# Attention, then a low-rank mixer and an MLP: where the mixing factor is loaded from, how the gains reach the q copy, and the order of the first batch

## The chip, the cores and the metric

The kernel runs on one core of a Trainium2 chip. The metric is the device time of one execution in microseconds (us), median of several runs. Every run in this document was in the fast state; even so the mean granted clock of single executions lies between 0.987 and 1.000, which matters below. A profile is of one execution; its span is some 1.8 us shorter than the time. Ratios are the mean time of one kernel's fast runs over that of the kernel before's fast runs in the same rounds, so they are not quite the ratio of the medians quoted beside them.

PE is TensorE, DVE is VectorE, ACT is ScalarE, POOL is GpSimd, SP is SyncE; SPq and POOLq are their instruction queues. A "group" is four heads (loads of q, k and v), a "pair" two heads; a batch has 12 heads, so 3 groups and 6 pairs. Tile names in the profiles: `ph` and `po` are the two matmuls of the MLP, `pm` and `px` the mixing.

## The reference

```python
q_n, k_n = rmsnorm(q, g_q), rmsnorm(k, g_k)            # q, k, v: 8 x 12 x 448 x 64
attn = softmax(q_n @ k_n^T / sqrt(64)) @ v
x = attn with the heads side by side                   # 8 x 448 x 768
u = x + (x^T @ U @ V)^T                                # U: 448 x 32, V: 32 x 448
out = u + relu(u @ w_ch1) @ w_ch2                      # 768 x 3072, 3072 x 768
```

Inputs and outputs are float32; the kernel multiplies in bfloat16.

## The kernel before

PE is to be busy all the time: while the MLP of batch b runs, the attention of batch b+1 is woven between its matmuls. Before the first MLP there is nothing to weave with, so batch 0 has a hand-made order, the "head": a string of words, each one step (`SC20` scores of pair 2, block 0; `X20` its exponential; `V20` its product with v; `N20` the normalization; `R2`, `q2`, `S2` reduce, rsqrt and scaling; `sq` squares; `w10` the first of six chunks of w_ch1; `late` the block below). Every engine does its steps in that order.

```python
def setup_late():                                      # all on POOL
    nc.gpsimd.tensor_copy(Us, Uf...)                   # U and V to bfloat16
    nc.gpsimd.tensor_copy(V4..., Vf...)
    nc.gpsimd.tensor_copy(Vsh[:, 0, 0:64], V4[:, 384:448])
    nc.gpsimd.tensor_copy(Vsh[:, 1, 64:128], V4[:, 0:64])
# [...]
def load_mix(part):
    if part == "U":
        nc.gpsimd.dma_start(Uf, moe_U...)
    else:                                              # V four times, one below the other, by one DMA
        nc.gpsimd.dma_start(Vf, bass.AP(moe_V.tensor, moe_V.offset, [[0, 4], [S, rank], [1, S]]))
# [...]
def take_q(p, pt):                                     # PSUM to SBUF, times the product of the gains
    nc.vector.tensor_scalar(blocks(p)[:, :, 0], pt[:, 0], gg, None, OP.mult)
# [...]  the middle of the head: V is sent at ld:V; late, sq5 and cast1 stand in a row on POOL; V20 needs cast1
#   ... X01 SC02 ld:V T1:0 X02 Eq1 ... X21 S3 T3:0 R4 q4 SC22 N00 X22 V10:1 late SC23 Eq3
#   V11:2 sq5:p Ek3:v cast1 SC30 S4 pU:0 N11 X23 SC31 X30 T4:2 SC32 N10 X31 V20:1 ...
# [...]  in the attention of batch 1 (pairs 6 to 11), for the pairs of batch 2:
if p == 9:   add(0, touch, 6); add(0, load, 6); add(0, load_v, 6)        # group 6 = pairs 12, 13
if p == 10:  add(0, squares, 12); add(0, squares, 13)                    # POOL
if p == 11:  add(0, reduce, 12); add(0, reduce, 13)                      # DVE, behind the first head of pair 10, ahead of the other three of pairs 10 and 11
```

(The last three lines are the effect of a longer set of conditions.) The weights are six chunks of w_ch1, then six of w_ch2 (three of its first half, three of its second), all sent by POOL, 0.79 MB each as written.

Of the kernel before, what the change touches and what calls it, by code (L numbers as in the profile page):

```python
# [17 lines left out]
def kernel(  # L18
# [60 lines left out]
    V4 = consts.tile([P, S], BF16, name="V4")  # L79
    Vsh = consts.tile([P, 2, P], BF16, name="Vsh")  # L80
    gg = consts.tile([P, 1], FP32, name="gg")
    grow = consts.tile([1, 4, D], FP32, name="grow")
    one = consts.tile([1, 1], FP32, name="one")
    eps = consts.tile([SP, 1], FP32, name="eps")
    rk0 = consts.tile([SP, 8], FP32, name="rk0")
    NE, NV, NQ, NWARM = 2, 3, 4, 11
    Es = [consts.tile([SP, 2, PAD + NJ * S + PAD], BF16, name=f"E{i}") for i in range(NE)]
    vas = [consts.tile([SP, HG, NJ, D + 1], BF16, name=f"va{i}") for i in range(NV)]

# [26 lines left out]
    def setup():  # L116
        nc.vector.memset(xss[1], 0.0)
        nc.gpsimd.memset(eps, D * 1e-6)
        nc.gpsimd.memset(one, 1.0)
        for i, g in enumerate((g_q, g_k)):  # L120
            nc.gpsimd.dma_start(grow[:, i], g.rearrange("(o d) -> o d", o=1))
        nc.gpsimd.memset(shift, 0.0)
        make_identity(nc, ident)
        for t in Es:
            nc.gpsimd.memset(t[:, :, 0:PAD], 0.0)
            nc.gpsimd.memset(t[:, :, PAD + NJ * S:], 0.0)
        for t in vas:
            nc.gpsimd.memset(t[:, :, :, D:D + 1], 1.0)
        for t in qkTs:
            nc.gpsimd.memset(t[:, SQK:], 0.0)  # L130
        nc.gpsimd.memset(Vsh, 0.0)

    def setup_late():
        nc.gpsimd.tensor_copy(Us, Uf.rearrange("p (j r) -> p j r", j=NJ))
        nc.gpsimd.tensor_copy(V4.rearrange("r (j p) -> r j p", j=NJ), Vf.rearrange("r (p j) -> r j p", j=NJ))
        nc.gpsimd.tensor_copy(Vsh[:, 0, 0:64], V4[:, 384:448])
        nc.gpsimd.tensor_copy(Vsh[:, 1, 64:128], V4[:, 0:64])

    def gain_row():

        nc.vector.tensor_tensor(grow[:, 2:4], grow[:, 0:1].to_broadcast([1, 2, D]),
                                grow[:, 1:2].to_broadcast([1, 2, D]), OP.mult)

    def gain(column):

        nc.tensor.matmul(column, grow[:, 2:4].rearrange("o h d -> o (h d)"), one, start=True, stop=True)

    def load_mix(part):
        if part == "U":
            nc.gpsimd.dma_start(Uf, moe_U.rearrange("(p j) r -> p (j r)", j=NJ))  # L150
        else:
            nc.gpsimd.dma_start(Vf, bass.AP(moe_V.tensor, moe_V.offset, [[0, 4], [S, rank], [1, S]]))

    def setup_U(pU):
        for par in range(2):
# [32 lines left out]
    def load(t):  # L188
        for a in range(2):
            for s in range(2):  # L190
                load_pair(nc.sync, t, s, a)
# [49 lines left out]
    def blocks(p):  # L241
        return qkTs[p % NQ][:, 0:SQK].rearrange("p (j s r) -> p j s r", j=NJ, s=2)
# [4 lines left out]
                                ident[:SP, :SP])  # L247

    def take_q(p, pt):
        nc.vector.tensor_scalar(blocks(p)[:, :, 0], pt[:, 0], gg, None, OP.mult)  # L250

    def take_k(p, pt, copy=nc.vector.tensor_copy, js=slice(0, NJ)):
        copy(k_side(p)[:, 0:SQK].rearrange("p (j s r) -> p j s r", j=NJ, s=2)[:, js, 1], pt[:, 1, js])
# [261 lines left out]
    def begin(hcs, dcs):  # L515
# [15 lines left out]


    HEAD = """
        sq00:a sq01:a R00 q00 R01 rk00 q01 sq1:a gg G ld:U Sq00 Sq01 GC rk01 Tq0:0 F4:1 sq2:a
        Sk0 Tk0:1 F2:2 Ek0:a R1 Sl0 Tl0:2 q1 Eq0 SC00 El0:v sq3:p S1 cast0 R2 X00 SC01 F2:0 X01
        SC02 ld:V T1:0 X02 Eq1 SC03 F2:1 Ek1:v SC10 F1:0 q2 X03 X10 S2 SC11 sq4:p T2:0 R3 X11 q3
        SC12 V01:1 Ek2:v X12 SC13 V00:2 Eq2 SC20 w10 X13 SC21 w11 N01 X20 X21 S3 T3:0 R4 q4 SC22
        N00 X22 V10:1 late SC23 Eq3 V11:2 sq5:p Ek3:v cast1 SC30 S4 pU:0 N11 X23 SC31 X30 T4:2
        SC32 N10 X31 V20:1 Ub:a X32 R5 w12 Eq4 Ek4:v SC33 V21:0 X33 MT1:2 N20 q5 t1:v SC40 MT0:1
        V30:2 cast2 t0:a X40 N21 SC41 S5 V31:0 N30 SC42 N31 T5:1 X41 SC43 w13 X42 w14 sq6:p  # L540
        MU1:0 Ek5:v MU0:2 Eq5 SC50 u1:v MT2:1 X43 u0:a X50 R6 SC51 MT3:0 t3:v V40:2 SC52 sq7:p
        t2:v X51 X52 MU3:0 SC53 N40 V41:1 B10 w15 X53 R7 w20 MU2:2 N41 B11 q6 B00 S7 V51:1 u3:a
        w21 u2:a V50:0 N51 N50 MT4:2 B01 S6 B12 t4:a B02 MT5:0 MU4:1 t5:a B03 MU5:0 B13 u4:v B04
        B14 u5:v B05 B15
    """

    def head():
# [18 lines left out]
        def op(name, p, n, how):  # L566
# [11 lines left out]
            elif name == "q" and p == 0:  # L578
                nc.scalar.activation(rs0[n], rs0[n], AF.Ln, bias=eps)
                nc.scalar.activation(rs0[n][:, 0:4], rs0[n][:, 0:4], AF.Exp, scale=-0.5)  # L580
            elif name == "rk":
                nc.scalar.activation(rk0[:, 4 * n:4 * n + 4], rs0[n][:, 4:8], AF.Exp, scale=-0.5)
            elif name == "q":
                rsqrt(p, 2 if p == 6 else 1)
            elif name == "S":
                scale(p)
            elif name in ("Sq", "Sk", "Sl"):
                if 0 not in qkns:
                    qkns[0] = norm.tile([SP, NJ, 4, D], BF16, tag="qkn", name="qkn", bufs=3)
                if name == "Sq":  # L590
                    nc.vector.tensor_tensor(qkns[0][:, :, n], raw0(0)[:, :, n],
                                            rs0[n][:, 0:4].rearrange("p j -> p j ()").to_broadcast([SP, NJ, D]),
                                            OP.mult)
                else:
                    js = FIRST if name == "Sk" else REST
                    rk = rk0.rearrange("p (h j) -> p j h ()", j=NJ)[:, js]
                    nc.gpsimd.tensor_tensor(qkns[0][:, js, 2:4], raw0(1)[:, js],
                                            rk.to_broadcast([SP, js.stop - js.start, 2, D]), OP.mult)
            elif name == "T":
                hold(("T", p), how, SQK, BF16)  # L600
                for s in range(2):
                    turn(p, s, turned(("T", p)))
                del qkns[p]
            elif name == "Tq":
                hold(("Tq", 0), how, SQK, BF16)
                turn(0, 0, turned(("Tq", 0)))
            elif name in ("Tk", "Tl"):
                hold((name, 0), how, SQK, BF16)
                turn(0, 1, turned((name, 0)), (0,) if name == "Tk" else range(1, NJ))
            elif name == "Eq":  # L610
                take_q(p, turned(("T" if p else "Tq", p)))
            elif name in ("Ek", "El"):
                js = slice(0, NJ) if p else FIRST if name == "Ek" else REST
                take_k(p, turned(("T" if p else "T" + name[1], p)), copies[how], js)
            elif name == "SC":
                scores(p, (n,))
            elif name == "X":
                expo(p, n)
            elif name == "V":
                products(p, n, hold(("V", p, n), how, 4 * (D + 1)).rearrange("p (i d) -> p i d", i=4))  # L620
            elif name == "N":
                normalize(p, n, held["V", p, n].rearrange("p (i d) -> p i d", i=4))
            elif name == "MT":
                mix_to(hold(("MT", p), how, P), 0, slice(p * P, (p + 1) * P))
            elif name == "t":
                copies[how](t_of(0)[:, p * P:(p + 1) * P], held["MT", p])
            elif name == "MU":
                mix_u(p, hold(("MU", p), how, 384))
            elif name == "u":
                copies[how](u_tile(0)[:, p, :], held["MU", p])  # L630
            elif name == "pU":
                setup_U(hold("pU", how, 8 * rank).rearrange("p (a i r) -> p a i r", a=2, i=4))
            elif name == "Ub":
                copies[how](Ub, held["pU"].rearrange("p (a i r) -> p a i r", a=2, i=4))
            elif name == "B":
                begin(range(2 * p, 2 * p + 2), (n,))
            elif name == "F":
                heat(p, banks[int(how)])
            elif name == "w":
                if p == 1:  # L640
                    load_w1(n)
                else:
                    load_w2(0, n)
            elif name == "cast":
                cast_v(p)
            elif name == "gg":
                gain_row()
            elif name == "G":
                gain(warm[:, 1, 0:1])
                heat(2, warm[:, 0, :])  # L650
            elif name == "GC":
                nc.scalar.copy(gg, warm[:, 1, 0:1])  # L652
            elif name == "ld":
                load_mix(how)
            elif name == "late":
                setup_late()

# [13 lines left out]
    with tc.manual_schedule():  # L671
# [7 lines left out]
        load(1)  # L679
        load_v(0)  # L680
        load(2)
        load_v(1)
        load_v(2)
        setup()
# [68 lines left out]
```

## Time and profile before

| | us |
|---|---|
| time, median of 4 runs beside the changed kernel | 598.01 (597.3 to 598.39) |
| span of the profiled execution | 596.9 |
| first exponential starts | 10.62 |
| last exponential of batch 0 ends | 40.7 |
| first ph matmul (MLP of batch 0) | 46.52 |
| first mixing matmul of batch 1 | 95.11 |
| first ph matmul of batch 1 | 109.11 |

How to read it: PE is busy 97% of the span, so only what happens before its steady state can be shortened. The "first ph matmul" of a batch is a milestone in PE's order. The prediction below shows the lines for the stretch up to 46.52. The q copy, by its tile (least, median and most ns; first and last start):

```profile
L250 DVE TENSOR_SCALAR qkT<-bank,gg x6: 441/442/442, 9.6 to 35.4; 128x448 bf16<-128x448 bf16 x6
```

Second, the DMA queues in the two stretches from 75 to 85 us (q0: POOL's queue, the weights; q1: SP's; packets, MB, share):

```profile
q0 software_dynamic: 1237, 0.94, 120.9%
q1 hardware_dynamic: 43, 0.04, 3.3%
...
q1 hardware_dynamic: 1459, 1.42, 83.7%
q0 software_dynamic: 172, 0.12, 16.3%
```

From 75 to 80 the weights have the engines almost to themselves; by 80 they are all but through, and only then SP's loads of group 6 (sent at 78.23 to 80.23) run, almost alone: its last k lands 5.4 us after being sent, at 85.1. In this kernel the two miss each other.

### The profile page before, as it was taken

How to read it: one execution, taken by the hardware profiler on the slowest of the kernel's cores; microseconds unless marked ns; L12 is line 12 of the kernel's file. 1: busy time of each engine (PE TensorE's matmuls, PEld its weight loads, DVE VectorE, ACT ScalarE, POOL GpSimd, SP SyncE). 2: the span in 40 equal slices, each digit the busy share in tenths (PEclk: the TensorE clock that was granted, in tenths of full speed). 3: DMA queues.
4: the chain of work that ended last, by engine and by line, in shares of the span. 5: the costliest groups of instructions: out<-in, count | busy, mean ns of one | idle time of the engine just before them, and what ended most of it. 6: DMA issues, size and time to landing. Idle time of an engine off the chain costs nothing.

```text
span 596.9 us, 11275 instructions
## 1 busy us (share of the span) xinstructions
PE 581.9 (97%) x4699; PEld 319.4 (54%) x4720; DVE 297.4 (50%) x602; ACT 263.6 (44%) x426; POOL 126.5 (21%) x112
## 2 busy tenths in 40 slices
PE   7699999999999999999999999999999999999996
PEld 2465556444565555544565556544465555654563
DVE  5775867555443566454453665545454362521111
ACT  6666541566503772175610875056630476112200
POOL 6693132333030330220230131303303000000000
PEclk9979999999999999999999999999999999999999
DMA  9999993944343544553253652832445310150021
GB/s 285 253 234 238 205 231 109 235 138 126 71 137 87 138 138 130 125 136 87 77 166 68 156 142 46 201 96 84 137 124 99 69 25 9 41 94 0 1 54 53
DMA packets 107859, 72.27 MB, mean 121 GB/s; under 512 B 56676, under 2 KB 104164, under 8 KB 107808
## 3 DMA queue, kind: packets, MB, share of 16 engines
q1 hardware_dynamic: 96016, 61.30, 40.3%
q0 software_dynamic: 11232, 9.73, 10.0%
q8 instruction: 37, 0.61, 0.4%
q10 hardware_dynamic: 560, 0.52, 0.3%
q14 instruction: 14, 0.11, 0.1%
HBM read 56.78 MB, written 11.01 MB: 114 GB/s over the span
## 4 chain that ended last, share of the span: by engine, by line
PE 93%; DMA 3%; POOL 1%; ACT 1%; issue 0%; DVE 0%; SPq 0%; POOLq 0%; DVEq 0%
PE po L413 37%; PE ph L393 36%; PE sc L278 7%; PE o L291 7%; DMA Vf<-in_moe_V_dram 2%; DMA qk<-in_k_dram 2%; PE px L363 1%; PE bank L291 1%; PE sc L523 1%; PE pm L338 1%; POOL w2b L217 1%; ACT E L283 0%; PE pt L246 0%; ACT hT L396 0%; POOL va L203 0%
## 5 line engine op out<-in xcount | busy, mean ns | idle before, releaser
L283 ACT ACTIVATE E<-sc 112x896 bf16<-112x896 f32 x192 | 172.1, 914 | 162.8 <-PE sc L278 162.8
L413 PE MATMUL po<-w2b,hT 128*128 128x384 bf16 x1344 | 238.3, 326 | 0.0
L413 PEld LDWEIGHTS <-hT 128*128 128x128 bf16 x1344 | 126.4, 98 | 87.6 <-issue 9.2
L393 PEld LDWEIGHTS <-w1b 128*128 128x128 bf16 x1128 | 102.7, 98 | 105.2 <-issue 19.3
L217 POOL TENSOR_TENSOR sq<-qk 112x1024 f32<-112x1024 f32 x42 | 79.3, 1896 | 312.0 <-DMA qk<-in_k_dram 233.3
L393 PE MATMUL ph<-uB,w1b 128*128 128x512 bf16 x556 | 131.4, 379 | 1.1
L396 ACT ACTIVATE hT<-ph 128x512 bf16<-128x512 f32 (+1 forms) x122 | 66.8, 547 | 106.8 <-PE ph L393 106.4
L393 PE MATMUL ph<-uA,w1b 128*128 128x384 bf16 x552 | 100.3, 326 | 0.1
L398 DVE TENSOR_SCALAR hT<-ph 128x384 bf16<-128x384 f32 (+1 forms) x66 | 41.1, 622 | 90.5 <-PE ph L393 90.3
L291 PEld LDWEIGHTS <-E 112*128 112x128 bf16 x1536 | 62.1, 99 | 19.9 <-issue 6.8
L278 PE MATMUL sc<-qkT 64*128 64x448 bf16 x376 | 55.7, 361 | 2.0 <-ACT E L283 1.1
L291 PE MATMUL o<-va,E 112*128 112x65 bf16 x1344 | 56.9, 194 | 0.0
L231 DVE TENSOR_TENSOR qkn<-qk,rs_bank 112x1024 bf16<-112x1024 f32 x45 | 54.5, 1213 | 2.8 <-ACT rs_bank L226 2.3
L220 DVE TENSOR_REDUCE rs_bank<-sq 112x16 f32<-112x1024 f32 x43 | 52.6, 1223 | 3.4 <-ACT gg L652 1.1
L303 DVE RECIPROCAL rec<-o 128x4 f32<-128x4 f32 x84 | 15.2, 181 | 72.6 <-PE o L291 72.2
L417 DVE TENSOR_TENSOR osb<-po,xe 128x384 f32<-128x384 f32 x32 | 17.7, 557 | 40.2 <-PE po L413 39.6
L417 DVE TENSOR_TENSOR osb<-po,xo 128x384 f32<-128x384 f32 x24 | 13.4, 558 | 43.4 <-PE po L413 43.4
L278 PEld LDWEIGHTS <-qkT 64*128 64x128 bf16 (+1 forms) x384 | 13.4, 95 | 35.5 <-issue 28.8
L203 POOL CAST va<-vt 112x1024 bf16<-112x1024 f32 x23 | 23.9, 1042 | 1.2 <-DMA vt<-in_v_dram 1.2
L269 ACT ACTIVATE qkT<-qkT,gg 128x448 bf16<-128x448 bf16 x36 | 23.9, 663 | 0.0
L365 DVE TENSOR_TENSOR xe<-px,xe 128x384 bf16<-128x384 f32 x32 | 17.7, 554 | 10.1 <-PE px L363 7.1
L311 DVE TENSOR_TENSOR xe<-o,rec 64x64 bf16<-64x64 f32 x84 | 18.3, 218 | 0.7
(95 smaller groups left out, 215.3 us busy)
## 6 DMA issues: line engine op xcount, KB each, us to landing
qk<-in_q_dram SPq DMA_DIRECT2D x44, 256.0 KB, 4.3
vt<-in_v_dram SPq DMA_DIRECT2D x22, 512.0 KB, 5.8
qk<-in_k_dram SPq DMA_DIRECT2D x43, 256.0 KB, 4.7
w1b<-in_moe_w_ch_dram POOLq DMA_DIRECT2D x6, 768.0 KB, 17.9
w2b<-in_moe_w_ch_dram POOLq DMA_DIRECT2D x6, 768.0 KB, 32.4
out_dram<-osb SPq DMA_DIRECT2D x8, 336.0 KB, 2.8
out_dram<-osb SPq DMA_DIRECT2D x8, 288.0 KB, 3.0
out_dram<-osb SPq DMA_DIRECT2D x8, 240.0 KB, 2.8
```

Source lines behind the costliest of these rows:

```text
L203: nc.gpsimd.tensor_copy(vas[t % NV][:, :, :, 0:D], v_of[t][0:SP].rearrange("p h (j d) -> p h j d", d=D))
L217: nc.gpsimd.tensor_tensor(dst, src, src, OP.mult)
L220: nc.vector.tensor_reduce(rs_of(p).rearrange("p (s h j) -> p s h j", s=2, h=2)[:, :, hs], sqs[p].rearrange("p (s h j d) -> p s h j d", s=2 ...
L231: nc.vector.tensor_tensor(qkns[p].rearrange("p j g d -> p g j d"), qk_of[t][0:SP, a].rearrange("p s h (j d) -> p (s h) j d", d=D), rs_of(p ...
L278: nc.tensor.matmul(sc[0:n, hh, 0:S], flat[pp, c:c + n], blocks(p)[pp, :, 0], start=True, stop=True)
L283: nc.scalar.activation(Es[p % NE][:, :, PAD + kc * S:PAD + (kc + 1) * S], scs.pop((p, kc))[0:SP, :, 0:S], AF.Exp, scale=float(D) ** 0.5)
L291: nc.tensor.matmul(o[:, i, :], E[:, hh, c:c + P], va[:, hl, kc, :], start=(kc == 0), stop=(kc == NJ - 1))
L393: nc.tensor.matmul(ph, w1b[:, dc, hc * P:(hc + 1) * P], u[:, dc, :], start=(dc == 0), stop=(dc == KD - 1))
L396: nc.scalar.activation(hT[:, hc, 0:n], ph, AF.Relu)
L398: nc.vector.tensor_relu(hT[:, hc, 0:n], ph)
L413: nc.tensor.matmul(po, hT[:, hc, i * P:(i + 1) * P], w2b[:, half, hc], start=(hc == 0), stop=(hc == KH - 1))
L417: nc.vector.tensor_add(osb[:, hs], po, xt[i][:, hs])
```

## The change

Its intent: have V there when POOL wants it, take the small product of the gains off DVE, and reorder the head around that.

```diff
-    def load_mix(part):                                # U right after the set-up, V at ld:V, POOL's queue
-        ...one DMA each...
+    def load_mix():
+        nc.sync.dma_start(Uf, moe_U.rearrange("(p j) r -> p (j r)", j=NJ))
+        for i in range(4):
+            nc.sync.dma_start(Vf[i * rank:(i + 1) * rank], moe_V)
@@ the loads at the start
         load(2)
+        load_mix()
         load_v(1)
@@ the gains: two columns (two matmuls, one ACT copy) instead of the product of two rows on DVE
-        nc.vector.tensor_scalar(blocks(p)[:, :, 0], pt[:, 0], gg, None, OP.mult)
+        nc.vector.tensor_scalar(blocks(p)[:, :, 0], pt[:, 0], gcol[:, 0:1], gcol[:, 1:2], OP.mult, OP.mult)
@@ setup_late
+        nc.gpsimd.tensor_tensor(gg, gcol[:, 0:1], gcol[:, 1:2], OP.mult)      # for later batches
@@ HEAD: another order (cut): squares of pairs 2, 3, 4 and 5 on POOL; late and sq5 ahead of V01;
@@ cast1 ahead of S3, so that SP sends v3 and v4 ahead of the loads of group 4; one more warm-up
@@ matmul at the start, the two behind the gains gone, and the later ones placed anew
```

More of the change, by code (lines that the diff above doesn't have):

```diff
@@ L81 @@
     gg = consts.tile([P, 1], FP32, name="gg")
-    grow = consts.tile([1, 4, D], FP32, name="grow")
+    grow = consts.tile([1, 2, 2, D], FP32, name="grow")
+    gcol = consts.tile([P, 2], FP32, name="gcol")
     one = consts.tile([1, 1], FP32, name="one")
@@ L85 @@
     rk0 = consts.tile([SP, 8], FP32, name="rk0")
-    NE, NV, NQ, NWARM = 2, 3, 4, 11
+    NE, NV, NQ, NWARM = 2, 3, 4, 12
     Es = [consts.tile([SP, 2, PAD + NJ * S + PAD], BF16, name=f"E{i}") for i in range(NE)]
@@ L120, in setup @@
         for i, g in enumerate((g_q, g_k)):
-            nc.gpsimd.dma_start(grow[:, i], g.rearrange("(o d) -> o d", o=1))
+            nc.gpsimd.dma_start(grow[:, i], bass.AP(g.tensor, g.offset, [[0, 1], [0, 2], [1, D]]))
         nc.gpsimd.memset(shift, 0.0)
@@ L137, in setup_late, with gain @@
         nc.gpsimd.tensor_copy(Vsh[:, 1, 64:128], V4[:, 0:64])
-    def gain_row():
-        nc.vector.tensor_tensor(grow[:, 2:4], grow[:, 0:1].to_broadcast([1, 2, D]),
-                                grow[:, 1:2].to_broadcast([1, 2, D]), OP.mult)
-    def gain(column):
-        nc.tensor.matmul(column, grow[:, 2:4].rearrange("o h d -> o (h d)"), one, start=True, stop=True)
-    def load_mix(part):
-        if part == "U":
-            nc.gpsimd.dma_start(Uf, moe_U.rearrange("(p j) r -> p (j r)", j=NJ))
-        else:
-            nc.gpsimd.dma_start(Vf, bass.AP(moe_V.tensor, moe_V.offset, [[0, 4], [S, rank], [1, S]]))
+    def gain(columns):
+        for i in range(2):
+            nc.tensor.matmul(columns[:, i:i + 1], grow[:, i].rearrange("o h d -> o (h d)"), one, start=True, stop=True)
+    def load_mix():
+        nc.sync.dma_start(Uf, moe_U.rearrange("(p j) r -> p (j r)", j=NJ))
+        for i in range(4):
+            nc.sync.dma_start(Vf[i * rank:(i + 1) * rank], moe_V)
     def setup_U(pU):
@@ L533 @@
     HEAD = """
-        sq00:a sq01:a R00 q00 R01 rk00 q01 sq1:a gg G ld:U Sq00 Sq01 GC rk01 Tq0:0 F4:1 sq2:a
-        Sk0 Tk0:1 F2:2 Ek0:a R1 Sl0 Tl0:2 q1 Eq0 SC00 El0:v sq3:p S1 cast0 R2 X00 SC01 F2:0 X01
-        SC02 ld:V T1:0 X02 Eq1 SC03 F2:1 Ek1:v SC10 F1:0 q2 X03 X10 S2 SC11 sq4:p T2:0 R3 X11 q3
-        SC12 V01:1 Ek2:v X12 SC13 V00:2 Eq2 SC20 w10 X13 SC21 w11 N01 X20 X21 S3 T3:0 R4 q4 SC22
-        N00 X22 V10:1 late SC23 Eq3 V11:2 sq5:p Ek3:v cast1 SC30 S4 pU:0 N11 X23 SC31 X30 T4:2
-        SC32 N10 X31 V20:1 Ub:a X32 R5 w12 Eq4 Ek4:v SC33 V21:0 X33 MT1:2 N20 q5 t1:v SC40 MT0:1
-        V30:2 cast2 t0:a X40 N21 SC41 S5 V31:0 N30 SC42 N31 T5:1 X41 SC43 w13 X42 w14 sq6:p
-        MU1:0 Ek5:v MU0:2 Eq5 SC50 u1:v MT2:1 X43 u0:a X50 R6 SC51 MT3:0 t3:v V40:2 SC52 sq7:p
-        t2:v X51 X52 MU3:0 SC53 N40 V41:1 B10 w15 X53 R7 w20 MU2:2 N41 B11 q6 B00 S7 V51:1 u3:a
-        w21 u2:a V50:0 N51 N50 MT4:2 B01 S6 B12 t4:a B02 MT5:0 MU4:1 t5:a B03 MU5:0 B13 u4:v B04
-        B14 u5:v B05 B15
+        sq00:a R00 sq01:a q00 R01 q01 rk00 rk01 Sq00 G Sk0 Sq01 GC Tq0:0 Sl0 sq2:p Tk0:1 F1:2
+        Tl0:2 sq3:p sq1:a Eq0 R1 Ek0:a SC00 F3:0 El0:v q1 cast0 S1 X00 SC01 F2:0 R2 sq4:p SC02
+        T1:0 w10 X01 SC03 F3:1 X02 q2 Eq1 X03 Ek1:v w11 S2 SC10 F1:0 SC11 X10 T2:0 R3 SC12 late
+        sq5:p X11 V01:1 Ek2:v Eq2 SC13 cast1 V00:0 q3 N01 X12 X13 w12 SC20 S3 X20 w13 SC21 T3:1
+        R4 SC22 X21 sq6:p q4 V11:2 X22 SC23 Eq3 Ek3:v N00 V10:1 cast2 SC30 X23 S4 pU:0 N10 SC31
+        N11 X30 X31 T4:1 R5 Ub:a SC32 V20:2 Eq4 SC33 X32 Ek4:v X33 q5 w14 N20 V21:0 N21 MT0:1
+        SC40 X40 MT1:2 SC41 t1:a V31:0 t0:v MU0:1 S5 N31 X41 u0:v SC42 T5:2 X42 MT2:0 Eq5 SC43
+        V30:1 Ek5:v SC50 X43 R6 t2:a MU1:2 SC51 X50 sq7:p N30 V40:0 X51 SC52 X52 u1:v MT3:1
+        MU2:2 SC53 N40 X53 w15 V41:0 t3:v B10 R7 MU3:1 q6 u2:a u3:a N41 B00 V51:0 V50:2 B11
+        MT4:1 w20 B01 B12 S6 t4:a N51 MU4:0 N50 MT5:1 w21 t5:a u4:a B02 B13 MU5:1 B03 u5:a S7
+        B14 B04 B15 B05
     """
@@ L645, in op @@
                 cast_v(p)
-            elif name == "gg":
-                gain_row()
             elif name == "G":
-                gain(warm[:, 1, 0:1])
-                heat(2, warm[:, 0, :])
+                gain(warm[:, 1, 0:2])
             elif name == "GC":
-                nc.scalar.copy(gg, warm[:, 1, 0:1])
-            elif name == "ld":
-                load_mix(how)
+                nc.scalar.copy(gcol, warm[:, 1, 0:2])
             elif name == "late":
```

## The prediction

> **What bounds the kernel now.** I read the page first. TensorE (PE) is busy for 97% of the span, so nothing outside PE's own work and its few gaps can be worth much. The slices show where the exceptions lie: PEclk is below 9 only in the third slice (about 30 to 45 us).
>
> ```profile
> PE 581.9 (97%) x4699; PEld 319.4 (54%) x4720; DVE 297.4 (50%) x602; ACT 263.6 (44%) x426; POOL 126.5 (21%) x112
> ...
> PEclk9979999999999999999999999999999999999999
> ```
>
> Next I asked for the busy time of each engine in stretches of 5 us over the start. Columns: stretch, length, busy us of PE, PEld, DVE, ACT and POOL (instructions), granted clock, DMA share, GB/s. PE loses time from 20 to 30 us; from 25 to 40 us its clock is reduced, to half in one row. From 10 to 20 us ACT and DVE are each busy for over 4.6 of every 5 us. DMA has no pause.
>
> ```profile
> 10.00:15.00 5.00, 4.12 (x30) 1.80 (x32) 4.65 (x8) 4.78 (x10) 4.45 (x4) 1.00 1.10 348
> 15.00:20.00 5.00, 4.26 (x74) 2.92 (x72) 4.83 (x9) 4.74 (x9) 2.96 (x4) 1.00 1.13 298
> 20.00:25.00 5.00, 3.08 (x51) 2.12 (x48) 3.14 (x8) 4.62 (x8) 1.55 (x4) 1.00 1.16 220
> 25.00:30.00 5.00, 2.28 (x34) 1.80 (x33) 2.48 (x5) 0.71 (x1) 5.00 (x5) 0.69 1.19 239
> 30.00:35.00 5.00, 5.00 (x61) 3.17 (x58) 3.05 (x8) 3.32 (x7) 4.99 (x5) 0.50 1.18 239
> 35.00:40.00 5.00, 5.00 (x62) 2.80 (x62) 4.22 (x9) 4.10 (x7) 5.00 (x6) 0.79 1.18 246
> ```
>
> The chain of waits over the same stretch (start, length, what) names the cause. POOL sends for V at 13.35, V lands at 23.34, and POOL then does the V cast, two shifted copies, a squares product and the cast of the next v, which PE needs.
>
> ```profile
> 13.35 9.99 DMA Vf<-in_moe_V_dram
> 23.34 0.05 issue
> 23.39 0.97 POOL V L135
> ...
> 24.42 0.24 POOL Vsh L136
> 24.66 0.18 POOL Vsh L137
> 24.84 1.09 POOL w2b L217
> ...
> 26.64 1.04 POOL va L203
> 27.68 0.04 issue
> 27.72 1.04 PE bank L291 x16
> ```
>
> The list of waits gives both ends: POOL idle for 5.4 us, PE for 4.2 us (its last matmul ended at 23.56, the next began at 27.72).
>
> ```profile
> POOL V L135 <- DMA Vf<-in_moe_V_dram: 5.4, 1, 5.4
> PE bank L291 <- POOL va L203: 4.2, 1, 4.2
> ```
>
> From 46.52 us, where the first MLP proper (the ph tile) starts, PE is busy without gaps that matter. So a change of the head (batch 0 before that point) moves the end by as much as it moves this start.
>
> **What the Trainium skill says.** (1) "TensorE: Matmul & The Clock Gate", its section on why this matters for your kernels, asks for no PE-idle gaps over about 3 us, because one idle window sends the clock back to half. The trace agrees: after a gap of 4.16 us the clock is 0.50 from 30 to 35, and a group of 16 values matmuls takes 0.99 us in the chain there, 0.62 later in the head. (2) The same page (engine queue depths) has GpSimd in strict order. The trace agrees: Us, ready since 10.8 us, is cast at 17.65, and behind V everything stands. (3) "DMA: Bandwidth & Descriptors", rules for kernel authors: an outermost zero-stride dim of c copies confines a DMA to at most c engines. V's old pattern leads with 4 copies. V took 10.0 us for 224 KB, but a 256 KB load sent at 13.05 took 10.5 us on the other queue, so this trace does not show that the pattern cost anything; the backlog alone could explain it. (4) The same page says that all issuing engines share the same 16 DMA engines. So moving V to SyncE moves no work away from them; what it can buy is an earlier place.
>
> **The change part by part.**
>
> V and U on SyncE: five issues placed after the loads of group 2, before v of group 1, at some 8.5 to 11 us. The neighbours tell the landing: the last k load before them was sent at 8.11 and took 7.0 us (15.1); the v behind them 8.86 plus 7.7 (16.6). The 0.28 MB of U and V at the 350 GB/s of that stretch is 0.8 us, so V should land at about 16, and loads behind it 0.8 us later.
>
> POOL, walked in its new order (the order listing confirms it): two k scalings once rk01 is there (6.5 to 7.7), squares of pair 2 when its k has landed (8.95 to 10.85; it was on ACT), squares 3 to 12.75, cast of v0 to 13.7, squares 4 to 15.5, two w1 issues of 0.88 to 17.3, then the late block: gg, U, V and two copies, about 1.9 us, to 19.2. V, at about 16, is there: no wait. Squares 5 end at 21.1 instead of 26.7, the v1 cast at 22.1 instead of 27.7. PE needs that cast after the last exponential of pair 2, itself near 21.6. **The 4.16 us gap should go.**
>
> Cold clock: from 27.72 to 36.89 the chain holds 9.17 us of PE pieces. At warm durations from the same trace these are 4 values groups x 0.62, 5 scores x 0.30, 2 mixes x 0.17, one set of transposes 0.40 and 2 u groups x 0.33, together 5.4 us. So **3.8 us** went to the half clock. With the gap, the bound on PE's side is 4.16 + 3.8 = 8.0 us.
>
> Gains: without DVE's product (0.28 us, and 0.7 us in which PE waited for it) the columns come some 1 us sooner; an extra column matmul (its weight load about 0.18 us) costs less than that. The q copy was 442 ns over 448 columns; a second per-partition factor in the same pass should leave it there (my estimate; this trace has no such form). The first exponential is still behind q1, so behind squares of pair 1 (to 8.47) and a 1.23 us reduce: about 10.2 instead of 10.62, 0.4 us.
>
> Can ACT and DVE follow? ACT needs 24 exponentials at 0.83 us in line, 20.0; four pairs of rsqrt at 0.36 to 0.4, 1.5; Ub and two small casts, 0.8: 22.3 us from 10.2, the last exponential ending at 32.5. DVE has about as much: five reduces (1.23), five scalings (1.21), five pairs of copies (0.8), eight normalizations (0.55) and small things. Walking both in order, with R2 gating q2, R5 gating q5 (25.1) and SC50 at 29.4, I get the last exponential ending at 33.1 (40.7 before). After it come the last values, R7, S6, two normalizations, mix 5, t5, u5, four matmuls of the MLP: DVE sets this tail, 5.3 us. The MLP starts at **38.4 instead of 46.5, 8.1 us sooner**. Two different sums thus give 8.0 and 8.1; they are not independent gains to be added.
>
> Weights then become the next edge. The landings before, issue plus time: w1 chunk 0 at 29.5, chunk 1 at 35.4 (16.8 + 18.6), chunk 2 at 42.3, chunk 3 at 46.8. First uses were 40.05, 46.52, 51.4 and 57.8. The margins are 10.5, 11.1, 9.1 and 11.0 us; shifting the uses by 8 leaves 1 to 3 us. DMA is full all along, so the earlier issue of chunks 2 and on (about 22 instead of 27.6) helps little, and the loads of v3 and v4, which follow the v1 cast, come 5 us sooner and share the engines. I allow 0.5 to 1 us for waits on weights or other unforeseen ones.
>
> Sum: 598.0 - 8.1 + 0.9 = 590.8 us, 1.2% less.
>
> **The rivals.**
> A. The weights bind: chunk 0, 1 or 2 lands later than its new use. For it: the margins above, and full DMA. Against it: the bytes to be moved by then are the same. It would cost 1 to 4 us of the gain (591 to 594); a wait over some 3 us would also cool PE's clock.
> B. V still comes late, or POOL, which takes over one squares product (1.9 us) from ACT, is the bound. For it: POOL is then busy almost without pause from 9 to 32 us. Against it: its walk has the cast only 0.5 us behind the need, and V has over 1 us in hand. Cost: 1 to 3 us.
> C. ACT and DVE bind harder than walked, since each must hold over 4.6 of 5 us all through. If the MLP starts at 41, the gain is 5.5 us: 592.5.
> D. More than 8 us: over 2% needs an MLP start before 34.7 us, which the 22.3 us of ACT work plus the 5.3 us tail from 10.2 exclude (37.8 at best), unless work of later batches also shrinks; nothing there is changed but the form of six q copies.
>
> **Range and chances.** The floor is 37.8 us for the MLP start (589.2), a little below for run-to-run spread: 588.6. The top takes A or C in a strong form with part of the gain lost: 593.8. Faster by over 2% is ruled out by the ACT sum unless I misread the head (0.03); slower by over 2% would need a new stall of 20 us (0.01).
>
> **What would show it.** In the changed profile: no wait of POOL for Vf; no PE gap over 3 us between 20 and 30 and a clock of 1.00 in each 5 us row of 20 to 40; the first exponential near 10.2, the last ending near 33; the first ph matmul near 38.5; the q copy near 442 ns; no, or short, waits of PE on w1b. From there the durations of both traces should be alike. The prediction is wrong if PE waits for w1b by several us, if a new POOL or DVE wait stands where V's was, or if the later batches differ.

## The result and the profile after

The changed kernel took **593.94 us** (593.57 to 594.06, 4 runs) beside 598.01: ratio 0.9932, 95% interval 0.9915 to 0.9949. That is 4.1 us less, 0.7%, where 7.2 were predicted, and just above the top of the range (593.8). The span went from 596.9 to 592.1.

The page and the stretches of the head after:

```profile
PE 579.1 (98%) x4699; PEld 317.9 (54%) x4720; DVE 296.5 (50%) x599; ACT 263.3 (44%) x427; POOL 127.4 (22%) x112
...
PEclk9999999999999999999999999999999999999999
```

```profile
20.00:25.00 5.00, 4.44 (x84) 3.19 (x81) 4.90 (x12) 4.95 (x10) 4.99 (x5) 1.00 1.17 255
25.00:30.00 5.00, 4.89 (x82) 3.23 (x79) 4.90 (x14) 4.77 (x9) 4.73 (x5) 1.00 1.18 241
30.00:35.00 5.00, 4.96 (x84) 3.41 (x85) 4.85 (x11) 4.72 (x9) 4.39 (x5) 1.00 1.18 245
35.00:40.00 5.00, 5.00 (x50) 3.02 (x47) 2.56 (x6) 1.47 (x5) 0.00 (x0) 1.00 1.18 245
```

The gap and the cold clock are gone. POOL's timeline (start, us) has V's cast without a wait:

```profile
17.81 0.30 POOL L136 CAST Us<-Uf 112x128 bf16<-112x128 f32 x1
18.05 0.99 POOL L137 CAST V<-Vf 128x448 bf16<-128x448 f32 x1
```

The milestones of both, each taken from the timelines of PE and ACT:

| | before | after | sooner by |
|---|---|---|---|
| first ph matmul of batch 0 | 46.52 | 39.67 | 6.85 |
| first po matmul of batch 0 | 77.02 | 70.30 | 6.72 |
| first mixing matmul of batch 1 | 95.11 | 90.08 | 5.03 |
| first ph matmul of batch 1 | 109.11 | 104.08 | 5.03 |
| span | 596.9 | 592.1 | 4.8 |

So the head gave 6.85 us, and **1.7 of them were given back between 70 and 90 us**, where the kernel's program is unchanged. The chain of waits shows the place (start, length, what):

```profile
71.58 0.37 SPq L183
...
73.03 11.28 DMA qk<-in_k_dram
...
84.43 1.90 POOL sq L214
...
86.35 1.23 DVE rs_bank L217
...
88.20 0.24 DVE xe L308
...
88.49 0.69 PE o L288 x16
```

SP sends the loads of group 6 at 71.58 to 73.6, 6.6 us sooner than before. The last k of them takes 11.28 us (5.4 before) and lands at 84.3, only 0.8 us before it landed in the kernel before. POOL squares pair 13 at once, DVE reduces it at once; but in DVE's order this reduce stands ahead of the normalization that frees PE's bank, and PE waits:

```profile
PE o L288 <- DVE xe L308: 1.5, 1, 1.5
```

The DMA queues in the two stretches from 75 to 85 us (q0: POOL's queue, the weights; q1: SP's; packets, MB, share), in the same form as those of before, say why the loads take twice as long: the weights still run beside them.

```profile
q0 software_dynamic: 735, 0.56, 70.8%
q1 hardware_dynamic: 685, 0.67, 49.4%
...
q0 software_dynamic: 683, 0.52, 65.6%
q1 hardware_dynamic: 790, 0.77, 54.7%
```

### The profile page after: what moved, and what is told of

Same layout as the page of the kernel before. It is cut to its first block, busy times and chain, and to the rows that moved or that the text cites. A ratio compares the mean times of both kernels' runs of the same rounds, so it can differ in the third digit from the quotient of the medians.

```text
span 592.1 us, 11276 instructions
## 1 busy us (share of the span) xinstructions
PE 579.1 (98%) x4699; PEld 317.9 (54%) x4720; DVE 296.5 (50%) x599; ACT 263.3 (44%) x427; POOL 127.4 (22%) x112
## 4 chain that ended last, share of the span: by engine, by line
PE 91%; DMA 3%; DVE 3%; ACT 1%; issue 1%; SPq 0%; POOL 0%; DVEq 0%; POOLq 0%; ACTq 0%
PE ph L390 37%; PE po L410 36%; PE sc L275 7%; PE o L288 7%; DMA qk<-in_k_dram 2%; PE px L360 1%; DVE rs_bank L217 1%; DMA qk<-in_q_dram 1%; PE bank L288 1%; DVE qkn L228 1%; PE sc L520 1%; PE pm L335 1%; ACT E L280 0%; SPq L183 0%; ACT hT L393 0%
## 5 line engine op out<-in xcount | busy, mean ns | idle before, releaser
L288 PEld LDWEIGHTS <-E 112*128 112x128 bf16 x1536 | 60.8, 98 | 18.0 <-issue 3.2
L414 DVE TENSOR_TENSOR osb<-po,xe 128x384 f32<-128x384 f32 x32 | 17.7, 557 | 40.2 <-PE po L410 39.6
L275 PEld LDWEIGHTS <-qkT 64*128 64x128 bf16 (+1 forms) x384 | 13.3, 94 | 36.5 <-issue 28.2
L362 DVE TENSOR_TENSOR xe<-px,xe 128x384 bf16<-128x384 f32 x32 | 17.7, 554 | 10.1 <-PE px L360 7.1
```

The lines of the kernel that those rows point to most:

```text
L275: nc.tensor.matmul(sc[0:n, hh, 0:S], flat[pp, c:c + n], blocks(p)[pp, :, 0], start=True, stop=True)
L288: nc.tensor.matmul(o[:, i, :], E[:, hh, c:c + P], va[:, hl, kc, :], start=(kc == 0), stop=(kc == NJ - 1))
L414: nc.vector.tensor_add(osb[:, hs], po, xt[i][:, hs])
```

## The experiments

Sixteen runs. **Theory**: V's late landing made the gap, and loading it sooner is worth 7 to 8 us of the head by the gap and the half clock; part is lost because PE, now sooner, asks for group 6 while DMA still has weights to move. **Rivals**: the new order or the columns made the gain; the cold stretch cost nothing; the loss is due to SP's changed order (v3 and v4 ahead of group 4), to DVE's order alone, or to slow small DMAs. As the first loads arrive at different moments in different executions (the first exponential starts between 10.05 and 13.21 us in these profiles), I compare distances between milestones: from the first exponential to the first ph matmul of batch 0 (the head), and from there to the first ph matmul of batch 1 (the first weave).

| run | time us (n) | ratio to before, 95% | head | first weave |
|---|---|---|---|---|
| before | 597.9 to 598.4 | 1 | 35.90 | 62.59 |
| changed kernel | 593.94 (4) | 0.9932 (0.9915 to 0.9949) | 29.13 | 64.41 |
| changed kernel again (e9) | 594.42 (6) | 0.9937 (0.9917 to 0.9957) | 29.13 | 64.37 |
| e1, V back on POOL | 597.76 (4) | 0.9991 (0.9972 to 1.001) | 34.95 | 62.76 |
| e2, V on SP, old order | 594.26 (4) | 0.9929 (0.9907 to 0.995) | 28.23 | 64.07 |
| e16, the same again | 593.78 (5) | 0.9927 (0.9915 to 0.9939) | 28.26 | 64.18 |
| e3, idle matmuls in the gap | 595.99 (4) | 0.9964 (0.9945 to 0.9983) | 32.67 | 63.22 |
| e4, one DMA for V | 594.69 (4) | 0.9937 (0.9916 to 0.9958) | 30.67 | 63.88 |
| e5, last w2 chunk later | 593.08 (5) | 0.9905 (0.9884 to 0.9926) | 30.46 | 64.24 |
| e6, group 4 before v3 | 594.19 (4) | 0.9933 (0.9911 to 0.9955) | 29.11 | 64.32 |
| e7, one factor | 593.59 (4) | 0.9921 (0.9899 to 0.9944) | 28.82 | 64.06 |
| e8, reduces at the end | 595.69 (4) | 0.9956 (0.9925 to 0.9986) | 29.12 | 64.73 |
| e10, reduces in the mixing | 594.79 (6) | 0.9947 (0.9925 to 0.9969) | 29.13 | 64.92 |
| e11, e2 with e10 | 594.07 (6) | 0.9936 (0.9914 to 0.9957) | 28.27 | 64.79 |
| e12, V early on POOL | 593.67 (6) | 0.9925 (0.9905 to 0.9945) | 28.20 | 63.10 |
| e13, e2 with w2 between | 593.90 (6) | 0.9936 (0.9922 to 0.9951) | 28.27 | 63.29 |
| e14, w2 between | 594.46 (6) | 0.9941 (0.9927 to 0.9956) | 29.53 | 65.06 |
| e15, e10 with PE's order kept | 593.32 (5) | 0.9927 (0.9914 to 0.994) | 29.47 | 64.11 |

All outputs are right. The single times of one kernel scatter by up to 4.3 us, so only differences of 2 us or more are told by the times here; smaller ones are told by the profiles or not at all.

Part of the scatter goes with the clock. Of the before runs beside e9 to e12, the one at 0.998 took 595.24 us, the ten at 0.987 to 0.993 took 597.45 to 599.58. The profiles show a second cold stretch, near the start and without a gap like that of the kernel before: in four of the eleven executions with the new order the clock falls to half, for some 3.4 us between 7.8 and 13.3 us in e9, e14 and e15, and for 6.8 us from 10.5 in e5; the six others with the old order show no such fall. With it e5's head is 1.3 us longer than the changed kernel's, although e5's edit changes nothing there, so a head read from one profile can be off by that much.

**e1: the changed kernel with V and U back on POOL's queue.**

```diff
-        load_mix()                        # on SP
+        ld:U and ld:V in the head again   # one POOL DMA each, V after cast0
```

> The changed kernel, but U and V go back to GpSimd's queue at their old places (V one DMA with four copies leading), so that the new order and the gain columns stand alone. Theory (the late V made the gap): V lands near 23 us, POOL waits for it about 4 us, PE has a gap of 3 to 4 us near 22 to 27, the clock falls to half, the first ph matmul comes at 45 to 46.5, the time is 597 to 599. Rival (the new order makes the gain, V would have been hidden in it): no gap over 1 us, first ph matmul by 41, time 593 to 594.5.

V took 10.0 us again, POOL waited 5.3 us for it, and the gap and the cold clock came back:

```profile
27.29 1.04 PE L292 MATMUL bank<-va,E 112*128 112x65 bf16 x16 [3.62 <-POOL va L204]
```

The time is that of the kernel before: the new order and the columns alone are worth nothing that the times can tell. (In the one profile the head is 0.95 us shorter than before.)

**e2 and e16: the kernel before with V and U on SP, and nothing else.**

```diff
-        ld:U and ld:V in the head
+        load(2); load_mix(); load_v(1)    # five DMAs on SP, as in the change
```

> The kernel before with one part of the change alone: U and V by five DMAs on SyncE's queue; old order, old gain. Theory (V's queue and place are nearly all of it): no wait of POOL for V, no cold clock, first ph matmul at 39 to 41, time 593 to 595. Rival (the order is needed for it): first ph matmul at 43 or later, time above 596.

> The run of U and V on SyncE with the old order again, on the chip of the three beside it, so that the effect of the w2 chunk alone can be read. Both theories: 593.5 to 594.8, PE's wait of about 1.3 us near 87, 64.1 us between the two first ph matmuls.

This one part has the whole effect (0.9929 and 0.9927, the change 0.9932 and 0.9937). Its head is even 0.9 us shorter than the changed kernel's, 28.23 against 29.13, and its first weave loses 1.5 us (1.8 in the changed kernel): PE waits 1.33 and 1.42 us near 87. Since SP's order is the old one here, the loss can't be due to v3 and v4 standing ahead of group 4.

**e3: the kernel before, V as late as ever, with 18 matmuls for nothing in the gap.**

```diff
-        SC32 N10 X31 V20:1
+        SC32 N10 X31 F9:1 F9:1 V20:1
```

> The kernel before, V as late as before, with 18 idle matmuls of 512 columns put in front of the values matmuls that wait for the v cast (they write a bank that is free then). The gap in useful work stays 4.2 us, but PE is busy in it. If the half clock cost what the prediction says (3.8 us): clock 1.00 in every 5 us row from 20 to 40, first ph matmul at 42.5 to 43.5, time 594 to 595.5. Rival (in the cold stretch PE was waiting for ACT and DVE anyway): first ph matmul at 45.5 or later, time 597 or more.

PE's timeline and the stretch that was at half clock before:

```profile
23.70 4.06 PE L508 MATMUL bank<-xe 128*128 128x512 bf16 x18
28.25 0.67 PE L291 MATMUL bank<-va,E 112*128 112x65 bf16 x16 [0.50 <-POOL va L203]
```

```profile
30.00:35.00 5.00, 4.92 (x79) 3.11 (x78) 4.84 (x12) 4.95 (x10) 4.99 (x5) 1.00 1.19 240
```

The values matmuls start as late as before, but take 0.67 us a group instead of 1.04. The head is 3.2 us shorter, the time 2.4 us (0.9964, interval clear of 1): work that produces nothing made the kernel faster, because the clock stayed up. So the half clock cost 3.2 us (the values start 17.4 us behind the first exponential here and 17.1 before, so perhaps 0.3 more), and the rest of e2's 7.67 (35.90 less 28.23), some 4.4, goes with the gap itself.

**e4: V by one DMA with four copies leading, on SP.**

```diff
-        for i in range(4):
-            nc.sync.dma_start(Vf[i * rank:(i + 1) * rank], moe_V)
+        nc.sync.dma_start(Vf, bass.AP(moe_V.tensor, moe_V.offset, [[0, 4], [S, rank], [1, S]]))
```

> The changed kernel with V by one DMA on SyncE's queue, four copies as the leading dimension, in place of four DMAs of 32 rows. Theory A (the pattern confines the DMA to four engines and makes it slow): issue to landing above 8 us, where the four took 3.9 to 6.2, and landing after 18 us, so that POOL waits; loads behind it late. Theory B (what cost was SyncE's issuing, 3.3 us for four small DMAs that move little, during which the engines run dry): SyncE gets on 2 us sooner, DMA moves more than 281 GB/s from 15 to 20 us, time equal or up to 1 us less.

Both theories were partly right. SP got on sooner: the four DMAs hold it for 3.31 us in the changed kernel, the one for 0.74, and v1 was sent at 10.48 instead of 13.96. But V, sent at 9.69, was only there when POOL had waited 0.9 us for it, at 18.7, some 9 us after being sent, where the four took 3.9 to 6.2. The head is 1.5 us longer, but the chain that ends in PE's wait there (1.59 us) does not lead back to V. It leads over DVE's reduce to POOL's square of pair 7 and to the k of that pair:

```profile
16.33 15.17 DMA qk<-in_k_dram
...
31.67 1.90 POOL sq L213
...
35.41 1.19 PE bank L287 x32
```

In the changed kernel this k was sent later, at 17.10, took 10.7 us and was there when POOL came to it. Why it took 15.17 us here is not shown. The time is not told apart (0.9937).

**e12: V's one DMA left on POOL, sent right after U.**

```diff
-        ... SC02 ld:V T1:0 ...
+        ... G ld:U ld:V Sq00 ...
```

> The kernel before with one issue moved: V's single DMA, four copies leading, stays on GpSimd's queue but is sent directly after U, near 5.5 us instead of 13.4. Theory A (its place in time is what mattered, not its queue or its pattern): V lands by 16, no wait of POOL for it, first ph matmul at 38.5 to 40, time 593.5 to 595. Theory B (GpSimd's queue is starved behind SyncE's loads, so that only SyncE's place helps): V lands after 19, POOL waits 1 us or more, first ph matmul after 41, time over 595.5.

V again took 10.0 us, from 5.3, and was there long before its cast. The head is as short as e2's (28.20) and the time the same (0.9925). What counted was that V is asked for early, not the queue and not the pattern. In this profile the first exponential is late (13.21). The chain names two reasons: the row of gains landed at 7.3 us (6.4 before), and two warm-up matmuls took 1.03 us at 8.27 where the kernel before took 0.60, so PE was at half speed. e13, without V in that place, got its gains later still (7.6), so nothing points to V; the times show no loss. PE waits only 0.34 us near 89 here; batch 0's MLP starts 2.7 us later than in e2.

**e7: one factor in the q copy.**

```diff
+                nc.scalar.activation(gg, gcol[:, 0:1], AF.Copy, scale=gcol[:, 1:2])
-        ... gcol[:, 0:1], gcol[:, 1:2], OP.mult, OP.mult)
+        ... gg, None, OP.mult)
```

> The changed kernel with one factor in the q copy: ScalarE multiplies the two columns once (one more instruction of about 0.15 us at 7.5 us). If the second per-partition factor is what took the q copy from 442 to 503 ns: 442 to 450 ns again, six copies in the head, at most 0.36 us less on VectorE; first ph matmul 0 to 0.4 us sooner than 39.67. Rival (the copy is slower for where it reads): it stays at 500 ns. The time is within 0.4 us of the changed kernel in both.

The q copy in the changed kernel, and then in this run:

```profile
L247 DVE TENSOR_SCALAR qkT<-bank,gcol x6: 501/502/509, 7.7 to 28.8; 128x448 bf16<-128x448 bf16 x6
```

```profile
L246 DVE TENSOR_SCALAR qkT<-bank,gg x6: 439/441/450, 7.8 to 28.4; 128x448 bf16<-128x448 bf16 x6
```

The second factor costs 60 ns each time. Five of them would make 0.30 us, as much as the head is shorter by here (28.82); but that is one profile, and which of them delay PE is not shown. The remaining 0.6 us to e2's head (28.23 and 28.26) may lie in the new order or in how the columns are made; I did not separate these two.

**e6: SP's old order, group 4 ahead of v3 and v4.**

```diff
-    ISSUE = {..., "S3": [(load, 4)], "cast1": [(load_v, 3), (load_v, 4)]}
+    ISSUE = {..., "S3": [(load, 4), (load_v, 3), (load_v, 4)]}
```

> The changed kernel with SyncE's order of the kernel before restored: loads of group 4 ahead of v3 and v4, which in the changed order stand first and make group 4 wait for the v1 cast (sent at 23.6 to 28.8 us instead of 14.8 to 18.9). Theory B (this blocking delays squares 8 and 9, then the last three weight chunks, and so the backlog that group 6 meets): group 6 lands at 82 or earlier, PE's wait near 87 gone, time 592 to 593. Theory A (the backlog is there whatever the order, as the run with V alone on SyncE and the old order suggests): squares 8 start before 38 instead of 40.9, but the k of group 6 still lands at 83 to 84.5 and the time stays at 593.5 to 594.2.

The k of group 6 took 11.21 us and landed at 83.7, PE waited 1.40 us, the first weave is unchanged (64.32). Theory A's reading holds in that, though not its detail: squares 8 came at 42.5, not before 38, because v3 was now late. The rival of SP's order falls, as in e2.

**e5: the last w2 chunk sent after the squares of pair 13.**

```diff
-        for i in range(3):
+        for i in range(2):
             load_w2(1, i)
@@ attention of batch 1, p == 10, behind squares(12) and squares(13)
+                    add(0, load_w2, 1, 2)
```

> The changed kernel, with the last of the six w2 chunks (0.79 MB written) sent only after the squares of pair 13, so that it is no longer in the queue when the loads of group 6 are sent near 71.6 us. Theory (what was given back later is the loads of group 6 meeting the backlog of weights): the last k load of group 6 lands at 81 to 83 instead of 84.3, PE's wait of 1.46 us near 87 shrinks below 0.5, the first ph matmul of batch 1 comes 1 to 1.6 us sooner than 104.1, time 592 to 593. Rival (the load is late for a reason of its own, as its place on SyncE): landing unchanged within 0.7 us, time as the changed kernel, 593.9.

```profile
73.80 6.94 DMA qk<-in_k_dram
...
82.75 0.78 POOL sq L214
...
84.59 11.03 DMA w2b<-in_moe_w_ch_dram
...
95.66 0.48 PE po L410 x2
```

With less of the weights in the queue, the two k of group 6 landed after 6.94 and 7.3 us, where the changed kernel's took 8.5 and 11.28, and PE's wait near 87 was gone. Part of that is this profile's late start: e12 and e4, whose MLP starts as late (41.41 and 40.90, here 41.49) with the chunk in its old place, have some 10 us for the last k and waits of only 0.34 and 0.17 us. e14 below starts nearly as the changed kernel does (40.15; 39.87 in e9) and settles it: 8.6 us where e9 has 11.2, and no wait near 87. So the backlog is what made it late. But the chunk, now beside the loads of group 7, took 11.03 us and PE waited 1.31 us for it. The wait changed its name. The times (592.24 to 593.25, and the profiled 595.69, with the cold stretch near its start) hint at a gain of some 0.9 us, within the interval of the changed kernel's; I don't count it.

**e14 and e13: the chunk between the two squares**, some 2 us sooner; e14 is the changed kernel with this, e13 is e2 with this.

```diff
+                    if p == 10 and a == 0:
+                        add(0, load_w2, 1, 2)      # after squares(12), ahead of squares(13)
```

> The changed kernel with only the last w2 chunk sent between the squares of pairs 12 and 13, some 2 us sooner than in the run where it stood after both and PE waited 1.3 us for it. Theory: the wait for w2 falls below 0.4 us, PE's wait near 87 stays away, batch 1's first ph matmul comes 62.7 to 63.3 us after batch 0's (64.4 in the changed kernel), time 592 to 593. Rival: as above, the wait for w2 stays at 0.8 us or more and the time is that of the changed kernel within 0.5 us.

> The version meant to beat both: the kernel before with U and V on SyncE (old order, old gain), and the last w2 chunk sent between the squares of pairs 12 and 13. Theory (the head's gain is kept if the loads of group 6 don't meet the backlog of weights, and the chunk still comes in time): the k of group 6 lands within 8 us of being sent, PE has no gap over 0.5 us from 80 to 103, the first ph matmul of batch 1 comes 62.6 to 63.2 us after that of batch 0, time 591.5 to 593. Rival (DMA is full whatever the order: what group 6 gains the chunk loses): PE waits 0.8 us or more for w2, 593.5 to 594.5.

In e14 PE waited even longer for the chunk, in e13 not at all, and only 0.5 us for DVE:

```profile
95.13 0.48 PE L410 MATMUL po<-w2b,hT 128*128 128x384 bf16 x2 [2.14 <-DMA w2b<-in_moe_w_ch_dram]
```

```profile
87.82 0.69 PE L290 MATMUL o<-va,E 112*128 112x65 bf16 x16 [0.54 <-DVE xe L310]
```

The chunk took 13.3 us in e14 and 10.2 in e13. In e13 the first weave is 0.9 us shorter than in e16 (63.29 against 64.18), yet the times, of the same chip and rounds, are 593.90 and 593.78. Nor is the 0.9 the chunk's alone: e13's first exponential came 1.4 us later (11.85 against 10.44), and by the theory a later PE meets less of the backlog. So it was not the better kernel that I had hoped for, and how long a chunk takes beside the loads of group 7 differs by more than what is to be won.

**e8: the reduces of pairs 12 and 13 at the end of batch 1's attention.**

```diff
-            (DVE: reduce 12, reduce 13 ahead of the last three normalizations of pairs 10 and 11)
+        if b == 1:                        # behind them
+            add(0, reduce, 12); add(0, reduce, 13); add(0, rsqrt, 12, 2)
```

> The changed kernel with the two reduces of pairs 12 and 13 moved behind the normalizations of batch 1 on VectorE, where they stand in front of one. The loads of group 6 land as late as before. Theory (the late load reaches PE only because VectorE keeps order: the reduce of pair 13 waits for its squares and holds up the normalization that frees PE's bank): k of group 6 still at about 84, PE's wait near 87 below 0.3 us, first ph matmul of batch 1 at 102.4 to 102.8 instead of 104.1, time 592 to 592.8. Rival (the scaling of pair 12 and the transposes behind it then come late and the wait moves to batch 2): time 593.5 or more, with a new PE gap between 104 and 125.

```profile
87.89 1.24 DVE rs_bank L217
...
89.22 1.23 DVE rs_bank L217
90.48 0.56 DVE osb L414
```

The wait near 87 is gone, as the theory says: the late loads reach PE only through DVE's order. But the two reduces now hold up the sum that frees a bank of the mixing, and PE waits 1.75 us at 91.09. The first weave is 64.73; the times are the most scattered of all the edited kernels (593.82 to 597.82).

**e10, e11 and e15: the reduces spread over the mixing.** e10 is the changed kernel with this, e11 is e2 with it, e15 is e10 with PE's order kept.

```diff
+            if b == 1 and i < 2:          # behind the first and the second tile of the mixing
+                items.append((0, lambda i=i: reduce(12 + i)))
```

> The changed kernel with the reduces of pairs 12 and 13 spread over the mixing of batch 1 on VectorE, one after each of the first two tiles, where VectorE has pauses. With both at the end of the attention the wait only moved to the mixing's first matmuls. Theory (what was given back is VectorE's order alone, the late load itself harms nothing): PE has no gap over 0.5 us from 80 to 104, first ph matmul of batch 1 63 us after that of batch 0 (64.4 before), time 1.2 to 1.6 us under the changed kernel. Rival (there is something else late in batch 1): a new gap of 1 us or more, time within 0.5 us of it.

> The kernel before with U and V on SyncE (as in the run with the old order) and the reduces of pairs 12 and 13 in the mixing. If both findings hold: first ph matmul at 38.5 to 39, that of batch 1 62.8 to 63.3 us later, time 592 to 593, under the changed kernel. Rival: the wait returns elsewhere, 594.

> As the run with the reduces in the mixing, but with PE's order kept exactly as in the changed kernel (in that run three items less in a list had moved two small matmuls, and a gap of 0.6 us near 65 with them). If that moved order was its whole loss: no gap near 65, batch 1's first ph matmul 63 us after batch 0's, time 592 to 593.3. If VectorE has no pause in the mixing for 2.5 us of reduces: from the first mixing matmul to batch 1's first ph matmul 15.3 us instead of 14.0, in all 63.9 to 64.2 us, time within 0.6 us of the changed kernel.

e10 and e11 missed, and were flawed: three items less in a list shifted two small matmuls in PE's order, and with them came a gap of 0.62 us near 65. e15 has PE's order exactly as in the changed kernel. There the gap near 65 is gone, but the mixing takes 15.34 us instead of 14.00, with this wait at its middle:

```profile
96.71 0.79 PE L360 MATMUL px<-t4b,V 128*128 128x384 bf16 x2 [0.46 <-DVE osb L418]
```

In the changed kernel DVE's longest pause among the operations of the mixing is 0.7 us, too short for a reduce of 1.2. e15's first weave, 64.11, is 0.3 us better than the changed kernel's, and its time (593.32) can't be told from it. e9, the changed kernel again, is the reference of e10 to e12:

> The changed kernel unaltered, so that the three beside it are compared with it on the same chip. Both theories: 593.5 to 594.5, PE's wait of about 1.4 us near 87, first ph matmul of batch 1 near 104.

PE's wait was 1.42 us there, as expected.

## Why the prediction was wrong

It gave 590.8 us, 588.6 to 593.8; measured were 593.94. Point by point, by its own steps:

- **V lands early, POOL doesn't wait, the gap goes: right.** V's last part was sent at 12.9, landed by 16.8, and was cast at 18.05 without a wait (predicted: 16 and about 17.7). e1 and e2 show that this is the whole gain.
- **The cold clock: right in kind, a little too large.** Predicted 3.8 us; e3 measured 3.2 to 3.5.
- **"Loads behind it 0.8 us later": wrong in size.** I counted V's bytes and not SP's time: each of the four small DMAs took SP 0.31 us to issue, but they left 1.0 us apart on average, since SP waited ahead of them for earlier loads to land (2.4 us in all in the list of SP's waits). So v1 went out 5.1 us later (13.96 against 8.86), group 3 3.5 to 4.7. DMA moved 286 GB/s from 10 to 15 us where it had moved 348. No wait of PE was traced to it in the head.
- **The q copy "should leave it there": wrong.** 442 ns became 502; e7 shows that it is the second factor.
- **The first ph matmul at 38.4: it came at 39.67,** 6.85 us sooner instead of 8.1. The first exponential came at 10.54 instead of 10.2, as the q of pair 1 landed 0.4 us later than I took from the trace before. The last exponential ended at 33.5 (predicted 33.1). The tail behind it took 6.2 us instead of 5.3: I had counted four MLP matmuls behind the last copy; PE had ten left from 38.05 on, and PE, not DVE, set that tail. From 23.08 on every piece of the chain of waits is PE's, so the walk through ACT and DVE had the wrong engine for the second half of the head.
- **The rivals.** A came nearest: DMA did take back part of the gain, but not by the weights' own landing, which I had tested against their first uses in the head and found to be in time; they were. B and D did not occur. C came true in half its size (39.67, not 41), and in the second half of the head by PE. (The floor of the range, 589.2, should read 589.3: 598.0 less 46.5 and plus 37.8; nothing rests on it.)
- **The step that failed** is the one that stands last in the part on what bounds the kernel: "a change of the head moves the end by as much as it moves this start", and with it the check "from there the durations of both traces should be alike". The stretch from 46.52 to 109.11 took 62.59 us before and 64.41 after. I had listed what the weights must reach and not what must be loaded beside them later. Group 6 is asked for at a point of PE's order, so it moved forward with PE; the weights' traffic is set by DMA and did not. In the kernel before the two missed each other by luck: the weights were through by 80 and the loads were sent at 78. An allowance of 0.9 us stood for 1.82.

In sum: 1.25 us less from the head, and 1.82 us lost in the first weave where 0.9 were allowed, together 2.2 us of the 3.1 by which the time missed. The profile of before that the prediction counts from is an execution of 598.7 us, 0.7 above its median. The rest, some 0.2 us, is the scatter of the times.

What stays open: whether DMA's volume is by then a bound that no order beats. e5 and e14 turned the wait for group 6 into one for a weight chunk, e8 and e15 into one for DVE; e13 has a first weave of 63.29, in part by its later start, but no shorter time. None of the sixteen runs is clearly faster than the changed kernel, and e2, with a much smaller edit, is its equal.

## What to carry to other kernels

Ask for what stands first in an in-order engine's queue long before it is needed: one late load of 0.2 MB held up everything behind it, and the idle PE (4.2 us) cost three quarters as much again in clock (3.2). Before you add up what a shorter start is worth, list the transfers that the later program asks for at fixed points of its own order: they move forward with it, into whatever traffic doesn't. And when you move a wait away, look for its next name before you believe the gain.

## What the Trainium skill lacked or had wrong

- "TensorE: Matmul & The Clock Gate", Part 1, has the clock back at full speed after at least one busy window of about 3.4 us, and does not say how many it can take. In the kernel before PE was busy without a pause from 27.72 us, and in rows of 2 us the clock stayed at 0.50 until 36 and was 0.72 from 36 to 38: some 9 us. In e1 PE went on at 27.29 and the clock was 0.50 until 34, 0.86 from 34 to 36: some 7 us. In e14 PE went on at 9.16 and the clock was 0.89 from 8 to 10, 0.50 to 12, 0.75 to 14 and then 1.00: half for 3.4 us. Falling agrees with the page: PE stopped at 23.56 and the clock fell within the row from 26 to 28.
- "VectorE: DVE Perf Modes", Scalar operands, tells that an instruction may read two [P, 1] operands, not what the second costs: here 60 ns, 442 to 502 for a copy of 128x448 from PSUM.
- "DMA: Bandwidth & Descriptors", rules for kernel authors, has a leading zero-stride dimension of c copies confine a DMA to at most c engines. The runs agree in direction: on SP some 9 us for the one DMA (e4), 3.9 to 6.2 for four of 32 rows; the engines used were not counted. Its section "Issuing engines are not separate DMA queues" has the time to initiate a DMA as usually small. The 0.31 us of one V issue agrees, but what it lacks is the wait: the four DMAs of 57 KB held SP for 3.31 us, as it waited for earlier loads to land.
- No page read says that an idle PE may be worth filling with matmuls for nothing in the middle of a kernel when a wait can't be removed: here 18 of them made it 2.4 us faster (e3).
